# Memory attention and gated convolution: convolution and x by token halves for both head groups side by side, one tap by way of ScalarE and GpSimd

## The chip, the cores and the metric

The kernel runs on one core of one Trainium2 chip. The metric is the device time of one execution in microseconds; the figure for a kernel is the median of its runs.

The core's engines work in parallel, each through a queue of its own in order: TensorE (PE in the profile; PEld is its weight load), VectorE (DVE), ScalarE (ACT), GpSimd (POOL) and SyncE (SP), which issues the transfers. They wait for one another through semaphores. TensorE writes to PSUM, from which VectorE and ScalarE read.

## The reference

Two stages, in float32. The first is an attention through 32 memory slots per head, the second a gated causal convolution of 5 taps with two projections:

```python
# batch 8, heads 8, seq 576, head_dim 64, 32 slots
a = phi - np.max(phi, axis=2, keepdims=True)
a = np.exp(a)
a = a / (np.sum(a, axis=2, keepdims=True) + 1e-09)
k_m = np.einsum('bhsm,bhsd->bhmd', a, k)
v_m = np.einsum('bhsm,bhsd->bhmd', a, v)
scores = scale * np.matmul(q, k_m.transpose(0, 1, 3, 2))
attn = softmax(scores)            # with the same 1e-09
x = np.matmul(attn, v_m)          # heads side by side: (8, 576, 512)
for k in range(5):
    gate_pre += conv_w[k][None, None, :] * xp[:, k:k + S, :]   # xp: x with 4 zero rows ahead
gate = 1.0 / (1.0 + np.exp(-gate_pre))
out = gate * (x @ w_val) @ w_out
```

## The kernel before

The 8 heads are two groups (`g`) of four; the 4 x 32 slots of a group fill the 128 partitions. The 576 tokens are two halves (`s`) of 288. One batch (`b`) passes these steps:

- `load_phi`, `phi_max` to `phi_exp`: the weights of the slots, as exponentials against a common maximum.
- `load_kv`, `slots`: k and v summed into the slots, 20 matmuls for a group; `slots_inv` and `slots_scale` divide by the sum into the tile `kvd`; `slots_turn` and `slots_place` transpose it to `kvT`.
- `scores`, `scores_turn`, `soft_max` to `soft_turn`: the softmax over 32 slots, turned to `pT` (slots on the partitions, tokens along the free dimension, 4 zero columns ahead). `soft_high` and `soft_low` split it into `pH` and `pL`, a rounded value and the rest, for matmuls in a narrower format.
- `val_rows`, `val_high`, `val_low`: v times `w_val`, split into `vwH` and `vwL`. `value(b, s, t)` makes x @ w_val for a half and a pair of heads `t` (0 to 3) by 6 matmuls.
- The gate, in one of two ways. `taps` and `conv(b, g)`: v is multiplied by the five tap weights, and 40 matmuls add the five shifted products in PSUM; `sigmoid` reads them. Or `keep_v` and `mix(b, g)`: 8 matmuls make x itself in PSUM (the tiles `cv`), and `tap(b, t, i)` adds its five shifted, weighted copies into the tile `gate`, tap 0 by ScalarE, taps 1 to 4 by VectorE, each over both halves (576 columns); `open_gate` is the sigmoid. The pairs of batch and group in `MIXED` go the second way: eight of sixteen.
- `gated` multiplies value and gate (tile `h`), `gated_high` and `gated_low` split the product, `project(b, s, n)` multiplies by `w_out` in 12 matmuls, `place` copies the result out of PSUM, `store` sends it.

A matmul of 32 rows by 64 columns takes one of eight parts of TensorE's array. `conv` places the heads of the second half shifted by one head, so that the eight products of (half, head) of a tap lie on eight parts. The heads of that half then lie in another order on the partitions: `swapped` groups need their columns of `vwH` and `vwL` again (`val_again`), and a second copy of `w_out` with its rows in that order (`woH[1]`, `woL[1]`, made by `wo_pair` with transfers inside SBUF). In `mix` both halves use the same four parts, one after the other.

The order of all steps on all engines is the list ORDER, written out in the source; a star behind a name sends the step to the other of its two engines. PSUM is two pools: `cv` (2 tiles of two banks, for `scores`, `conv` and `mix`) and `b` (4 tiles of one bank, for all else). A tile is given out again when its last reader is done. The k and v of a group have one buffer a group (`kvs`); `q` has one for a batch.

Of the kernel before, what the change touches and what calls it, by code (L numbers as in the profile page):

```python
# [721 lines left out]
```

## Time and profile before

| | |
|---|---|
| median of 3 runs | 268.93 us (268.8 to 272.24) |
| the profiled execution | 271.08 us, of which the span from its first to its last instruction 269.3 us |
| mean granted TensorE clock | 0.987 |
| busy: TensorE, VectorE, ScalarE, GpSimd | 250.1, 206.9, 140.5, 116.2 us |
| chain that ended last, by engine | TensorE 83%, transfers 10% |
| moved by transfers | 49.91 MB, 185 GB/s over the span |

All durations below are of the profiled execution and are read against its own 271.08 us. "Busy" counts time in which an engine executes an instruction; matmuls are pipelined, so the mean of one is its latency, and what a series costs is read from the chain of waits, where each piece is the time by which it moves the end. A tensor's line is the line of the helper that issued it: `high` and `low` are lines 216 and 219, `tap` 607 (ScalarE) and 611 (VectorE), `gated` 640, `conv` 577, `mix` 597, `project` 661, `value` 632, `scores` 449, `slots` 403.

### The profile page before, as it was taken

What the parts mean: (1) busy time and instruction counts of PE and PEld (TensorE: products, weight loads), DVE (VectorE), ACT (ScalarE), POOL (GpSimd) and SP (SyncE); (2) the same over time, 40 slices, a digit from 0 to 9 for tenths busy, and PEclk for the clock granted to TensorE, in tenths of its full rate; (3) what the DMA queues carried; (4) which work ended last, traced back from release to release, by engine and by line L of the source; (5) the groups of instructions that cost most, each with busy time, mean ns of one, the idle gap of its engine ahead of it and who ended that gap; (6) DMA issues with size and microseconds to landing.
All of it is one profiled execution on the core that took longest, in us unless ns stands there. A gap on an engine that the chain in (4) does not pass through costs nothing.

```text
span 269.3 us, 7274 instructions
## 1 busy us (share of the span) xinstructions
PE 250.1 (93%) x3096; PEld 216.0 (80%) x3096; DVE 206.9 (77%) x338; ACT 140.5 (52%) x245; POOL 116.2 (43%) x94
## 2 busy tenths in 40 slices
PE   0599959995999999999999999999999999999995
PEld 0387757793988887798789996999879878899994
DVE  2678978996759979789886777789577987898831
ACT  3726764762745558445685346636458565364210
POOL 4466613892921616323635540743237144461200
PEclk9999989998999999999999999999999999999999
DMA  6999987698681992099407268088143210102123
GB/s 203 407 357 355 320 339 247 156 240 234 249 318 60 333 352 99 15 325 347 167 12 217 103 223 267 0 287 334 44 142 127 77 56 2 44 2 88 46 88 131
DMA packets 13232, 49.91 MB, mean 185 GB/s; under 512 B 1673, under 2 KB 2185, under 8 KB 10257
## 3 DMA queue, kind: packets, MB, share of 16 engines
q1 hardware_dynamic: 13200, 49.46, 53.7%
q8 instruction: 24, 0.39, 0.6%
q14 instruction: 8, 0.06, 0.1%
HBM read 37.92 MB, written 9.44 MB: 176 GB/s over the span
## 4 chain that ended last, share of the span: by engine, by line
PE 83%; DMA 10%; issue 2%; ACT 2%; SPq 1%; DVE 1%; DVEq 0%; ACTq 0%
PE b L661 36%; PE b L632 18%; PE cv L577 8%; DMA kv<-in_kv_dram 8%; PE b L403 7%; PE cv L597 4%; PE cv L449 3%; PE b L532 2%; DMA e<-in_phi_dram 2%; PE b L433 2%; PE cv L226 1%; PE b L360 1%; SPq L259 1%; ACT hH L216 1%; DVE h L640 0%
## 5 line engine op out<-in xcount | busy, mean ns | idle before, releaser
L661 PE MATMUL b<-hL,woH 128*128 128x288 f32 x256 | 76.6, 299 | 0.0
L661 PE MATMUL b<-hH,woL 128*128 128x288 f32 x256 | 75.5, 295 | 0.0
L661 PE MATMUL b<-hH,woH 128*128 128x288 f32 x256 | 75.4, 294 | 0.0
L219 POOL TENSOR_TENSOR hL<-h,hH 128x576 fp32r<-128x576 f32 x22 | 32.6, 1488 | 60.0 <-ACT hH L216 32.2
L611 DVE SCALAR_TENSOR_TENSOR gate<-cv,cwP,gate 128x576 f32<-128x576 f32 x64 | 50.0, 813 | 5.9 <-ACT gate L607 4.8
L661 PEld LDWEIGHTS b<-hL,woH 128*128 128x128 f32 x256 | 48.0, 187 | 2.8 <-issue 1.0
L661 PEld LDWEIGHTS b<-hH,woH 128*128 128x128 f32 x256 | 48.2, 188 | 0.0
L661 PEld LDWEIGHTS b<-hH,woL 128*128 128x128 f32 x256 | 48.1, 188 | 0.0
L216 ACT COPY o<-b 128x288 f32<-128x288 f32 x48 | 18.7, 399 | 49.4 <-PE b L661 32.8
L640 DVE TENSOR_TENSOR h<-b,gate 128x288 f32<-128x288 f32 x64 | 27.9, 452 | 19.1 <-PE b L632 15.8
L632 PE MATMUL b<-pL,vwH 128*128 128x288 f32 x128 | 29.0, 308 | 0.0
L632 PE MATMUL b<-pH,vwH 128*128 128x288 f32 x128 | 27.3, 294 | 0.0
L632 PE MATMUL b<-pH,vwL 128*128 128x288 f32 x128 | 27.3, 294 | 0.0
L403 PE MATMUL b<-kv,e 128*32 128x129 f32 x640 | 21.8, 287 | 5.8 <-DMA kv<-in_kv_dram 3.1
L403 PEld LDWEIGHTS b<-kv,e 128*32 128x32 f32 x640 | 18.6, 139 | 8.9 <-issue 4.8
L632 PEld LDWEIGHTS b<-pL,vwH 128*128 128x128 f32 x128 | 20.1, 188 | 6.2 <-issue 2.4
L219 POOL TENSOR_TENSOR pL<-pT,pH 128x1152 fp32r<-128x1152 f32 x7 | 18.7, 2673 | 14.1 <-DVE pH L216 9.8
L577 PE MATMUL cv<-pT,taps 32*64 32x288 f32 x640 | 22.0, 410 | 0.1
L479 POOL TENSOR_TENSOR st<-st,mm 128x1152 f32<-128x1152 f32 x7 | 14.9, 2134 | 15.9 <-DVE mm L472 15.0
L216 ACT CAST hH<-h 128x576 fp32r<-128x576 f32 x21 | 13.9, 673 | 14.0 <-DVE h L640 14.0
L389 POOL TENSOR_TENSOR e<-e,mxa 128x1280 f32<-128x1280 f32 x7 | 17.2, 2464 | 8.7 <-ACT mxa L216 8.7
L632 PEld LDWEIGHTS b<-pH,vwL 128*128 128x128 f32 x128 | 20.5, 188 | 0.0
(87 smaller groups left out, 414.1 us busy)
## 6 DMA issues: line engine op xcount, KB each, us to landing
kv<-in_kv_dram SPq DMA_DIRECT2D x16, 1032.0 KB, 7.6
out_dram<-o SPq DMA_DIRECT2D x30, 288.0 KB, 2.4
q<-in_q_dram SPq DMA_DIRECT2D x7, 1152.0 KB, 8.4
e<-in_phi_dram SPq DMA_DIRECT2D x7, 640.0 KB, 6.4
kv<-in_kv_dram SPq DMA_DIRECT2D x16, 129.0 KB, 8.3
raw<-in_w_out_dram SPq DMA_DIRECT2D x4, 512.0 KB, 8.0
raw<-in_w_val_dram SPq DMA_DIRECT2D x4, 512.0 KB, 6.2
q<-in_q_dram SPq DMA_DIRECT2D x2, 576.0 KB, 8.1
```

The costliest lines, as they stand in the source:

```text
L216: eng.copy(out=out, in_=x) if eng is nc.scalar else eng.tensor_copy(out=out, in_=x)
L219: eng.tensor_tensor(out=out, in0=x, in1=hi.bitcast(F32), op=ALU.subtract)
L389: eng.tensor_tensor(out=t, in0=t, in1=mxa.unsqueeze(3).to_broadcast(list(t.shape)), op=ALU.subtract)
L403: nc.tensor.matmul(km[j * M:(j + 1) * M, 0:2 * D + 1], lhsT=e[:, g, j * M:(j + 1) * M, c], rhs=x[:, c, j, :], start=(c == 0), stop=(c == C ...
L449: nc.tensor.matmul(sc[j * M:(j + 1) * M, s, 0:HALF], lhsT=live["kvT", b, g][rows, 0, j * M:(j + 1) * M], rhs=live["q", b][rows, g, j, :], ...
L479: eng.tensor_tensor(out=st, in0=st, in1=spread(live["mm", b, g], st), op=ALU.subtract)
L577: nc.tensor.matmul(cv[t][x * D:(x + 1) * D, s, 0:HALF], lhsT=w[rows, i, :], rhs=p[rows, g, s * HALF + i:(s + 1) * HALF + i], start=(i == 0 ...
L597: nc.tensor.matmul(cv[t][x * D:(x + 1) * D, s, 0:PAD + HALF], lhsT=live["taps", b, g][rows, 0, :], rhs=pTs[b % 2][rows, g, s * HALF:(s + 1 ...
L611: nc.vector.scalar_tensor_tensor(out=gt, in0=x, scalar=w, in1=gt, op0=ALU.mult, op1=ALU.add)
L632: nc.tensor.matmul(vp[:, 0:HALF], lhsT=a[:, t // PG, n:n + P], rhs=p[:, g, s * HALF:(s + 1) * HALF], start=(i == 0), stop=(i == len(parts) ...
L640: nc.vector.tensor_tensor(out=h[:, i], in0=live["vp", b, s, t][:, 0:HALF], in1=live["gate", b, t][:, s], op=ALU.mult)
L661: nc.tensor.matmul(ps[:, 0:HALF], lhsT=w[:, t, n * P:(n + 1) * P], rhs=a[:, t % 2], start=(i == 0), stop=(i == len(parts) - 1))
```

## The change

`conv(b, s)` and `mix(b, s)` now take one half of the tokens for both groups, where they took one group for both halves. The second group's heads lie shifted by one on the array, for both halves alike; the arrays of weights are laid out in that order of heads ahead of the launch, so `swapped`, `val_again`, the second copies of `w_out` and `wo_pair` go. `kvd` is one tile for both groups, with v of both side by side: `mix` takes its weights there (`keep_v` goes), and three transposes a batch replace four. `tap(b, s, g, i)` works on one half, and as its two tiles of heads have weights of their own it issues two instructions of 288 columns. In the second group tap 1 goes another way: `part_tap` (ScalarE) writes it to a buffer of its own and `join_tap` (GpSimd, once VectorE) adds that to the gate. Twelve pairs of batch and half are mixed now; `conv` is left in 0.0, 0.1, 1.0 and 2.0. The last 64 tokens of k and v of both groups come by one transfer a batch (`load_rest`), and the rest by one for each group, in three buffers in turn. In batch 0 the scores and the softmax go by halves for both groups at once. `scores` has the same eight matmuls per group as before. The gate has 6 buffers instead of 5, `kvd` 3 instead of 2, `st` 2 instead of 1. ORDER is written anew.

```diff
-BUFS = {"raw": 4, "b": 4, "cv": 2, "kvd": 2, "kvT": 3, "st": 1, "vw": 4, "taps": 3, "gate": 5, "h": 3, "hh": 4, "o":
+BUFS = {"raw": 4, "b": 4, "cv": 2, "kvd": 3, "kvT": 3, "st": 2, "vw": 4, "taps": 3, "gate": 6, "h": 3, "hh": 4, "o":
...
-MIXED = {(1, 1), (2, 1), (3, 1), (4, 1), (5, 1), (6, 1), (7, 0), (7, 1)}
+KVS = 3
...
     def load_kv(b, g):
-        t = kvs[g]
-        nc.sync.dma_start(out=t[:, 0:C - 1], in_=kv[b, g, 0:S - KL].rearrange("(p c) n -> p c n", c=C - 1))
-        nc.sync.dma_start(out=t[0:KL, C - 1], in_=kv[b, g, S - KL:])
...
+        t = kvs[(b * G + g) % KVS]
+        nc.sync.dma_start(out=t, in_=kv[b, g])
...
+    def load_rest(b):
+        nc.sync.dma_start(out=rests[b % 2], in_=rest[b])
...
-    def wo_pair(i, g):
...
     def slots_scale(b, g):
...
+        kvd = own(("kvd", b), work, [P, G + 1, 2, D], F32, bufs=BUFS["kvd"])
...
+        for out, x in ((kvd[:, g], km[:, 0:D].unsqueeze(1).to_broadcast([P, 2, D])), (kvd[:, G, g], km[:, D:2 * D])):
...
-    def val_again(b, g, n):
...
-    def conv(b, g):
...
+    def conv(b, s):
+        cv = [psum.tile([P, PG, 512], F32, name="cv", bufs=BUFS["cv"]) for _ in range(G)]
         for i in range(KT):
-            for s in range(2):
+            for g in range(G):
                 for j in range(HG):
-                    rows = slice(j * M, (j + 1) * M)
-                    t, x = divmod((j - s) % HG, 2)
-                    nc.tensor.matmul(cv[t][x * D:(x + 1) * D, s, 0:HALF], lhsT=w[rows, i, :],
-                                     rhs=p[rows, g, s * HALF + i:(s + 1) * HALF + i],
+                    rows, x = slice(j * M, (j + 1) * M), (j + g) % 2
+                    nc.tensor.matmul(cv[g][x * D:(x + 1) * D, j // 2, 0:HALF], lhsT=live["taps", b, g][rows, i, :],
+                                     rhs=pTs[b % 2][rows, g, s * HALF + i:(s + 1) * HALF + i],
                                      start=(i == 0), stop=(i == KT - 1))
...
-    def keep_v(b, g):
...
-    def mix(b, g):
...
+    def mix(b, s):
+        cv = [psum.tile([P, PG, 512], F32, name="cv", bufs=BUFS["cv"]) for _ in range(G)]
+        for g in range(G):
             for j in range(HG):
-                rows = slice(j * M, (j + 1) * M)
-                t, x = divmod(j, 2)
-                nc.tensor.matmul(cv[t][x * D:(x + 1) * D, s, 0:PAD + HALF], lhsT=live["taps", b, g][rows, 0, :],
+                rows, x = slice(j * M, (j + 1) * M), (j + g) % 2
+                nc.tensor.matmul(cv[g][x * D:(x + 1) * D, j // 2, 0:PAD + HALF], lhsT=live["kvd", b][rows, G, g],
                                  rhs=pTs[b % 2][rows, g, s * HALF:(s + 1) * HALF + PAD], start=True, stop=True)
...
+    def tap(b, s, g, i):
+        gt = own(("gate", b, s, g), work, [P, PG, HALF], F32, bufs=BUFS["gate"])
+        for t in range(PG):
+            x, w = live["cv", b, s, g][:, t, i:i + HALF], cwP[:, i, g * PG + t:g * PG + t + 1]
+            if i == 0:
+                nc.scalar.activation(out=gt[:, t], in_=x, func=AF.Identity, scale=w)
+            else:
+                nc.vector.scalar_tensor_tensor(out=gt[:, t], in0=x, scalar=w, in1=gt[:, t], op0=ALU.mult, op1=ALU.add)
+
+    @step
+    def part_tap(b, s, g, i):
+        gt = work.tile([P, PG, HALF], F32, name="gate", bufs=BUFS["gate"])
+        for t in range(PG):
+            nc.scalar.activation(out=gt[:, t], in_=live["cv", b, s, g][:, t, i:i + HALF], func=AF.Identity,
+                                 scale=cwP[:, i, g * PG + t:g * PG + t + 1])
+        live["part", b, s, g, i] = gt
+
+    @step
+    def join_tap(b, s, g, i):
+        gt = live["gate", b, s, g]
+        eng = pick(nc.gpsimd, nc.vector)
+        eng.tensor_tensor(out=gt, in0=gt, in1=live["part", b, s, g, i], op=ALU.add)
```

Before, TensorE's queue around the `mix` of batch 3 (`mx` and `top` belong to the maximum of phi, `kvd` is transposed by `slots_turn`; the brackets name the engine that is waited for):

```order
L360 MATMUL b<-ident,mx 128x128 [waits DVE_49]
L360 MATMUL b<-ident,mx 128x128
L597 MATMUL cv<-pT_76,taps 64x292 [waits DVE_49]
L597 MATMUL cv<-pT_76,taps 64x292 x7
L376 MATMUL b<-ident,top 128x128 [waits DVE_49,Activation_49]
L376 MATMUL b<-ident,top 128x128
L433 MATMUL b<-ident,kvd 128x128 x2
L433 MATMUL b<-ident,kvd 128x128 [waits PE_49]
L433 MATMUL b<-ident,kvd 128x128
```

Now, the same queue around the second `mix` of batch 3; `kv` and `rest` are `slots` of batch 5, `q` the scores of batch 4, `pL` and `pH` belong to `value`:

```order
L395 MATMUL b<-rest_82,e 32x129 x3
L445 MATMUL cv<-q,kvT 32x288 [waits DVE_49]
L445 MATMUL cv<-q,kvT 32x288 x7
L395 MATMUL b<-kv_80,e 32x129 [waits DMAHW0_49]
L395 MATMUL b<-kv_80,e 32x129 x15
L395 MATMUL b<-rest_82,e 32x129 x4
L593 MATMUL cv<-pT_76,kvd 64x292 [waits DVE_49]
L593 MATMUL cv<-pT_76,kvd 64x292 x3
L593 MATMUL cv<-pT_76,kvd 64x292 [waits DVE_49]
L593 MATMUL cv<-pT_76,kvd 64x292 x3
L640 MATMUL b<-pL,vwH 128x288 [waits Activation_49,Pool_49]
L640 MATMUL b<-pL,vwH 128x288
```

The eight matmuls of a `mix` were four and four on the same parts of the array; now they are two fours on other parts, one for each `cv` tile, and each four waits for VectorE's last reading of its tile, here the transposes of the scores, with one `slots` as the work between.

Before, VectorE's queue around the taps of batch 4 (`vwL` and `vwH` are the split of v times w_val for batch 5):

```order
L611 SCALAR_TENSOR_TENSOR gate<-cv,cwP,gate 128x576 [waits Activation_49] x2
L611 SCALAR_TENSOR_TENSOR gate<-cv,cwP,gate 128x576 [waits DVE_49]
L216 COPY o<-b 128x288 [waits DMAHW5_49,DMAHW2_49,PE_49]
L611 SCALAR_TENSOR_TENSOR gate<-cv,cwP,gate 128x576 [waits DVE_49]
L611 SCALAR_TENSOR_TENSOR gate<-cv,cwP,gate 128x576
L611 SCALAR_TENSOR_TENSOR gate<-cv,cwP,gate 128x576 [waits DVE_49] x2
L611 SCALAR_TENSOR_TENSOR gate<-cv,cwP,gate 128x576
L640 TENSOR_TENSOR h<-b,gate 128x288 [waits PE_49,Activation_49]
L219 TENSOR_TENSOR vwL<-b,vwH 128x2x256 [waits Activation_49]
L216 CAST vwH<-b 128x2x256
L219 TENSOR_TENSOR vwL<-b,vwH 128x2x256 [waits DVE_49]
```

Now, the same queue at the two mixes of batch 5 (`pH` is the split softmax, `top` the maximum of phi):

```order
L359 TENSOR_REDUCE top<-b 128x2 [waits PE_49]
L606 SCALAR_TENSOR_TENSOR gate<-cv,cwP,gate 128x288 [waits Activation_49]
L606 SCALAR_TENSOR_TENSOR gate<-cv,cwP,gate 128x288
L606 SCALAR_TENSOR_TENSOR gate<-cv,cwP,gate 128x288 [waits DVE_49] x6
L606 SCALAR_TENSOR_TENSOR gate<-cv,cwP,gate 128x288 [waits Pool_49]
L606 SCALAR_TENSOR_TENSOR gate<-cv,cwP,gate 128x288
L606 SCALAR_TENSOR_TENSOR gate<-cv,cwP,gate 128x288 [waits DVE_49] x4
L648 TENSOR_TENSOR h<-b,gate 128x288 [waits PE_49,Activation_49]
L648 TENSOR_TENSOR h<-b,gate 128x288 [waits PE_49]
L648 TENSOR_TENSOR h<-b,gate 128x288
L606 SCALAR_TENSOR_TENSOR gate<-cv,cwP,gate 128x288 [waits PE_49,Activation_49]
L606 SCALAR_TENSOR_TENSOR gate<-cv,cwP,gate 128x288
```

Eight taps of 576 columns became fourteen of 288 for each `mix`; the last six of them stand behind a wait for GpSimd (the join), and the next `mix` follows behind three products.

Before, SP's queue ahead of the k and v of batch 2 (`kv` with a long and a short transfer for each group; `woL` and `woH` are the copies by `wo_pair`; `e` is phi):

```order
L249 DMA q<-in_q_dram 128x2304 [waits DMAHW7_49,PE_49]
L236 DMA e<-in_phi_dram 128x1280 [waits DMAHW0_49,PE_49,Activation_49]
L241 DMA kv_80<-in_kv_dram 128x2064 [waits DMAHW3_49,DMAHW1_49]
L242 DMA kv_80<-in_kv_dram 64x516 [waits DMAHW4_49,DMAHW2_49]
L339 DMA woL_91<-woL_90 64x1024 [waits Pool_49]
L341 DMA woL_91<-woL_90 64x512
L341 DMA woL_91<-woL_90 64x512 [waits DMAHW5_49]
L339 DMA woH_89<-woH_88 64x1024 [waits DMAHW6_49,Activation_49]
L341 DMA woH_89<-woH_88 64x512 [waits DMAHW7_49]
L341 DMA woH_89<-woH_88 64x512 [waits DMAHW0_49]
L241 DMA kv_78<-in_kv_dram 128x2064 [waits DMAHW1_49]
L242 DMA kv_78<-in_kv_dram 64x516 [waits DMAHW2_49]
```

Now, the same place:

```order
L257 DMA raw<-in_w_out_dram 128x1024 [waits DMAHW4_49,DVE_49]
L247 DMA q<-in_q_dram 128x2304 [waits DMAHW5_49,PE_49]
L237 DMA kv_80<-in_kv_dram 128x2064 [waits DMAHW6_49,DMAHW3_49,PE_49]
L242 DMA rest_81<-in_rest_dram 128x516 [waits DMAHW7_49]
L242 DMA rest_82<-in_rest_dram 128x516 [waits DMAHW0_49,PE_49]
L237 DMA kv_79<-in_kv_dram 128x2064 [waits DMAHW1_49]
L232 DMA e<-in_phi_dram 128x1280 [waits DMAHW2_49,Activation_49]
L682 DMA out_dram<-o 128x576 [waits Activation_49]
```

The copies that waited for ScalarE and GpSimd, with the load of the second group's k and v between them, are gone; both loads of batch 2 now go out ahead of the phi of batch 3 and of the first store.

## Rows read from the trace of the kernel before

**Rows 1.** The page, part 1: busy time, share of the span, instructions.

```profile
PE 250.1 (93%) x3096; PEld 216.0 (80%) x3096; DVE 206.9 (77%) x338; ACT 140.5 (52%) x245; POOL 116.2 (43%) x94
```

**Rows 2.** Busy us (instructions) by engine in five stretches; clock, DMA share, GB/s.

```profile
0.00:23.83 23.83, 13.39 (x113) 10.52 (x113) 14.10 (x23) 11.20 (x20) 12.72 (x19) 1.00 0.91 317
23.83:40.60 16.77, 13.90 (x276) 10.97 (x276) 14.63 (x27) 11.79 (x22) 7.27 (x8) 0.92 0.96 346
40.60:65.87 25.27, 22.49 (x322) 18.72 (x320) 21.29 (x33) 13.82 (x25) 16.03 (x13) 0.97 0.82 211
65.87:266.18 200.31, 200.29 (x2395) 175.74 (x2394) 156.85 (x256) 103.31 (x178) 80.15 (x55) 0.99 0.43 154
266.18:269.30 3.12, 0.00 (x0) 0.00 (x0) 0.00 (x0) 0.40 (x1) 0.00 (x0) 1.00 0.32 113
```

**Rows 3.** Chain of waits: start, us, what.

```profile
53.05 10.82 DMA kv<-in_kv_dram
...
65.87 2.15 PE cv L597 x16
...
123.58 1.14 PE cv L597 x16
...
131.92 1.13 PE cv L449 x32
...
137.28 2.62 PE cv L577 x80
...
153.73 0.22 PE b L433 x2
...
253.37 12.80 PE b L661 x96
```

**Rows 4.** TensorE in order of time, at the k and v of batch 2.

```profile
63.92 1.34 PE L403 MATMUL b<-kv,e 128*32 128x129 f32 x40 [2.78 <-DMA kv<-in_kv_dram]
```

**Rows 5.** Waits of SP's queue: us in total, times, longest.

```profile
SPq L339 <- ACT vwH L216: 7.5, 1, 7.5
```

**Rows 6.** Groups by form: count, busy us, mean ns, idle before and its releasers.

```profile
L611 DVE SCALAR_TENSOR_TENSOR gate<-cv,cwP,gate 128x576 f32<-128x576 f32 x64 | 50.0, 813 | 5.9 <-ACT gate L607 4.8
...
L219 POOL TENSOR_TENSOR hL<-h,hH 128x576 fp32r<-128x576 f32 x22 | 32.6, 1488 | 60.0 <-ACT hH L216 32.2 <-DVE hH L216 12.6 <-PE b L433 9.7
...
L640 DVE TENSOR_TENSOR h<-b,gate 128x288 f32<-128x288 f32 x64 | 27.9, 452 | 19.1 <-PE b L632 15.8 <-ACT gate L616 1.6 <-issue 1.0
...
L216 ACT COPY o<-b 128x288 f32<-128x288 f32 x48 | 18.7, 399 | 49.4 <-PE b L661 32.8 <-issue 15.7 <-ACT mxa L216 0.8
...
L607 ACT ACTIVATE gate<-cv,cwP 128x576 f32<-128x576 f32 x16 | 11.2, 741 | 10.6 <-PE cv L597 10.5
...
L616 ACT ACTIVATE gate<-gate 128x576 f32<-128x576 f32 x16 | 10.9, 687 | 5.6 <-DVE gate L611 5.5
...
L219 DVE TENSOR_TENSOR hL<-h,hH 128x576 fp32r<-128x576 f32 x10 | 7.6, 767 | 0.1
...
L424 DVE TENSOR_SCALAR kvd<-b,ri 128x256 f32<-128x256 f32 x9 | 4.3, 480 | 0.2
```

**Rows 7.** VectorE in order of time, three places: start, us, instruction, count.

```profile
106.82 0.69 DVE L219 TENSOR_TENSOR vwL<-b,vwH 128x512 fp32r<-128x512 f32 x1 [0.51 <-ACT vwH L216]
107.42 0.48 DVE L562 TENSOR_TENSOR taps<-cwB,kvd 128x320 f32<-128x320 f32 x1
...
206.23 0.45 DVE L640 TENSOR_TENSOR h<-b,gate 128x288 f32<-128x288 f32 x1
206.59 0.17 DVE L499 TENSOR_SCALAR ss<-ss 128x36 f32<-128x36 f32 x1
...
236.30 5.88 DVE L611 SCALAR_TENSOR_TENSOR gate<-cv,cwP,gate 128x576 f32<-128x576 f32 x8
```

**Rows 8.** Busy us by engine, as rows 2, in the last 20 us.

```profile
250.00:260.00 10.00, 10.00 (x76) 9.96 (x76) 6.28 (x14) 2.04 (x5) 1.43 (x1) 1.00 0.23 90
260.00:270.00 10.00, 6.16 (x47) 5.92 (x45) 1.59 (x4) 0.40 (x1) 0.00 (x0) 1.00 0.24 89
```

More of the change, by code (lines that the diff above doesn't have):

```diff
@@ L66 @@
-place.0.0.2 slots.2.0 phi_turn.3 slots_scale.2.1* wo_pair.0.0 val_again.1.1.vwH* mix.1.1 slots_inv.2.0 tap.1.2.0
-gated_low.0.1.1 slots_turn.2.1 phi_top.3 phi_spread.3 keep_v.2.1 slots_scale.2.0 soft_high.1* phi_lay.3 tap.1.2.1
-tap.1.2.2 slots_place.2.1 tap.1.3.0 tap.1.2.3 slots_turn.2.0 slots_place.2.0 tap.1.2.4 open_gate.1.2 tap.1.3.1
-tap.1.3.2 soft_low.1 wo_pair.1.1 project.0.1.1 place.0.1.1 load_q.2 project.0.1.0 load_kv.3.0 place.0.1.0 store.0.1.0
-tap.1.3.3 tap.1.3.4 open_gate.1.3 value.1.1.3 project.0.1.2 value.1.1.2 gated.1.1.3 taps.2.0 gated.1.1.2 place.0.1.2*
@@ L81 @@
-project.1.1.1 place.1.1.1 tap.2.2.1 phi_sub.4 phi_exp.4 project.1.0.0 project.1.1.0 place.1.1.0 tap.2.3.2 tap.2.3.3
-project.1.0.2 tap.2.3.4 open_gate.2.3 val_rows.3 place.1.0.2 val_high.3.1 store.1.0.1 tap.2.2.2 tap.2.2.3 tap.2.2.4
-open_gate.2.2 phi_max.5 soft_low.2 place.1.0.0 val_high.3.0 val_again.3.1.vwH conv.2.0 val_low.3.1 taps.3.0*
-val_again.3.0.vwH value.2.0.0 sigmoid.2.0 val_low.3.0 gated.2.0.0 sigmoid.2.1 value.2.0.1 gated.2.0.1 scores.3.0
-scores.3.1 scores_turn.3.0 scores_turn.3.1 soft_max.3 val_again.3.1.vwL* gated_high.2.0.0 slots.4.1 slots_inv.4.1
@@ L91 @@
-tap.3.2.3 tap.3.3.1 load_kv.5.1 tap.3.3.2 tap.3.3.3 store.1.1.0 phi_lay.5 slots_turn.4.1 keep_v.4.1 load_kv.5.0
-slots_turn.4.0 project.2.0.2 tap.3.2.4 project.2.1.3 place.2.0.2 val_again.3.0.vwL* soft_high.3 phi_sub.5
-slots_place.4.0 project.2.1.2 place.2.1.2 load_q.4 project.2.1.0 tap.3.3.4 scores.4.0 slots_place.4.1 scores.4.1
-phi_exp.5 scores_turn.4.0 scores_turn.4.1 soft_max.4 val_rows.4 store.2.0.0 place.2.1.3 store.2.1.1 val_high.4.1*
-place.2.1.0 project.2.1.1 val_high.4.0 taps.4.0* place.2.1.1 open_gate.3.2 soft_low.3 value.3.0.2 val_again.4.0.vwH
@@ L121 @@
-project.5.1.2 val_high.6.1 val_again.6.1.vwH* place.5.1.2 val_low.6.1 value.5.0.3 gated.5.0.3 value.5.0.0 gated.5.0.0
-project.5.1.0 value.5.0.1 soft_exp.6 soft_sum.6 phi_sub.7 phi_exp.7 gated.5.0.1 gated_high.5.0.0 project.5.1.3
-place.5.1.3 soft_inv.6 store.4.1.1 soft_mul.6* soft_turn.6 place.5.1.0* taps.6.0* project.5.1.1 val_again.6.1.vwL
-gated_high.5.0.1 slots.7.0 gated_low.5.0.0 gated_low.5.0.1* slots_inv.7.0 slots_scale.7.0 val_again.6.0.vwL*
-soft_high.6 mix.6.1 slots.7.1 tap.6.2.0 tap.6.2.1 slots_inv.7.1 tap.6.3.0 tap.6.2.2 tap.6.3.1 slots_turn.7.0 load_q.7
@@ new lines @@
+slots_scale.2.1* slots_turn.2 phi_turn.3 slots_place.2 value.1.1.0 join_tap.1.1.1.1 tap.1.1.1.2 tap.1.1.1.3
+tap.1.1.1.4 open_gate.1.1.0 phi_max.4 gated.1.1.1 load_kv.4.0 value.1.0.3 taps.1.0 taps.1.1 phi_top.3 conv.1.0
+sigmoid.1.0.0 load_kv.3.1 gated.1.1.0 sigmoid.1.0.1 taps.2.1 phi_turn.4 phi_top.4 gated_high.1.1.0 load_kv.3.0
+val_rows.2 val_high.2.1 scores.2.0 gated.1.0.3 scores_turn.2.0 scores.2.1 val_low.2.1 phi_spread.3 phi_lay.3 phi_sub.3
+scores_turn.2.1 soft_max.2 open_gate.1.1.1 project.0.1.0 project.0.1.1 place.0.1.0* val_high.2.0 val_low.2.0
```

400 lines of the change are left out of this document (205 added, 195 removed).

## The prediction

> **What bounds the kernel now.** I read the page's engine shares first [rows 1]: TensorE is busy 93% of the span, VectorE 77%, ScalarE 52%, GpSimd 43%. A share is an average, so next came a table of five stretches [rows 2]. From 65.87 to 266.18 us TensorE is busy 200.29 of 200.31 us at a granted clock of 0.99, and before that it has gaps. VectorE is busy 156.85 us of the same stretch, so it idles 43.5. The chain of waits [rows 3] says the same: from the first `mix` at 65.87 to the last projection that ends at 266.17 it runs through TensorE alone. So a microsecond taken from TensorE in that stretch is a microsecond of the end, as long as nothing else becomes late. Ahead of it the chain runs through loads, the last of them kv from 53.05 us on, and 3.1 us lie behind it.
>
> **TensorE, what goes.** In the chain one `conv` takes 2.62 us, one `mix` 1.14, and the scores of both groups 1.13 [rows 3]. A `conv` issues 40 matmuls and lays its eight (half, head) products of one tap on eight different parts of the array. A `mix` issues only 8, but its two token halves use the same four parts, so it takes two rounds of four. The scores are the model for what follows: 8 matmuls of 288 columns on eight parts, 1.13 / 2 = 0.57 us.
> - `conv` now takes both groups for one half: again 40 matmuls on eight parts, so again 2.62 us. In the stretch there were six (batches 1 to 6), now there are two (1.0 and 2.0): 4 x 2.62 = 10.5 us less.
> - `mix` now has both groups on eight parts: 0.57 us by the scores; the bounds are 0.52 (two of conv's ten rounds) and 1.14 (nothing gained). There were 8, now 12: 8 x 1.14 = 9.1 becomes 12 x 0.57 = 6.8, so 2.3 less.
> - The transposes of `slots_turn` fall from four to three a batch, 0.22 us for two [rows 3]: 0.11 a batch over some six batches, 0.7 less.
> Together 13.5 us, and the stretch needs 200.3 - 13.5 = 186.8 us of TensorE. Projections, values and slots keep their number.
>
> **The head.** I expect the first `mix` at about 63 instead of 65.87 us. TensorE waits 2.78 us at 61.1 for the kv of batch 2 [rows 4]. Its load goes out only at 53.05 [rows 3], since SP's queue stood 7.5 us at a copy of `woH` or `woL` that waited for ScalarE [rows 5]. Those twelve copies are gone, a kv tile has three buffers instead of one per group, and the order shows both kv loads of batch 2 ahead of anything that waits for late work. Against it: the first softmax needs the queries of both groups now, and they stand behind nine other loads. VectorE's work up to the first `mix` is about as long as before. I take the 2.8 us off; the bounds are 6 off and 1 on. What would be late next there is VectorE, busy 21.29 of 25.27 us in the stretch from 40.60 [rows 2].
>
> **VectorE, what comes.** This is the price of the change. A `mix` now serves one half of both groups: per mix 8 + 6 taps of 288 columns, since each tile of heads has weights of its own; 12 x 14 = 168 replace 64 of 576 columns (50.0 us) [rows 6]. No row shows a 288-column tap. Eight in a row of 576 take 5.88 us, 0.735 each [rows 7]. From below: half of that is 0.37. From above: the 288-column product `h`, which also reads PSUM, takes 0.452 by its mean [rows 6]. In between: `vwL`, 512 columns, starts 0.60 us ahead of its successor, and `h`, 288, 0.36 [rows 7], so a column costs 1.07 ns, and 0.735 - 288 x 1.07 ns = 0.43 us. I take 0.43, since it is from the tap itself: 168 x 0.43 = 72 us (62 to 76).
>
> [...]
>
> Less work elsewhere, by the order's counts: seven `hL` differences move from VectorE to GpSimd (7 x 0.767 = 5.4), nine `kvd` scalings of 0.48 become four smaller ones in the first two batches (about 3) [rows 6], and some ten small copies, casts and products go (0 to 5, I take 4). So VectorE needs 156.9 - 50.0 + 72 - 12 = 167 us in the stretch, where TensorE needs 186.8.
>
> **Does VectorE keep up?** Behind the last `mix` VectorE is nearly done while TensorE still has some 10 us more of work than VectorE has (the last 12.8 us are projections alone [rows 3]). So VectorE has 186.8 - 10 = 177 us for its 167: it may idle 10 us. Before it idled 43.5, of which 19.1 in front of `h`, mostly for TensorE's values [rows 6]; some 8 of the rest lay behind 250 us [rows 8]. If it still has to wait those 19.1, TensorE waits 9 us for gates; if less than 10, nothing. I take the middle, **4.5 us**; the bounds are 0 and 9.
>
> **ScalarE and GpSimd** are hidden. ScalarE gets 48 + 24 first and part taps in place of 16 (72 x 0.40 by the 288-column copy `o`, less 16 x 0.741: +17 us), 8 more sigmoids of 0.69 against 8 fewer behind `conv`, and the `kvd` scalings: some 125 of 187 us [rows 2, 6]. GpSimd gets 11 joins and 7 `hL`, 18 x 1.49 = 27 us, and loses the copies of `val_again` and `keep_v`: about 105 of 187. They count only as a delay: the second group's gate passes from ScalarE (tap 0 and the part tap) to GpSimd's join and back to six VectorE taps, while both `cv` tiles stay taken. In VectorE's order the first group's eight taps stand ahead of the wait for the join. They start behind the first of three pairs of ScalarE steps and end 0.8 + 3.4 = 4.2 us into the mix; the three pairs and the join take 2.4 + 1.5 = 3.9. So the join is covered, just, where nothing else is queued on GpSimd; its longest other work there is a `pL` or a subtraction, which could add 1 to 2 us to VectorE's waiting and is part of the bound of 9.
>
> **The sum.** Head 63.1, stretch 186.8 + 4.5, end 3.1: a span of 257.5 us. The profiled execution took 271.08 us with a span of 269.30, so 1.8 lie around it: 259.3. It was itself 0.8% above the median of 268.93: 259.3 x 268.93 / 271.08 = **257 us** on the scale of the median, 4.4% less. Its own range: 250 (VectorE hidden, head 3 us quicker) to 262 (VectorE waits as before).
>
> **Rivals.**
> A. VectorE becomes the bound. It keeps the whole of its old waiting outside the tail (35 us) beside 167 us of work: 202 instead of the 177 it has, so TensorE loses 25 us instead of 4.5. With half of that excess the span is 257.5 + 10 = 267.5 and the time 267. For it: in the stretch VectorE would be busy 89%, and it works its queue in order, so each wait for a value holds up the next taps. Against it: several batches are in work at once, and before the change it filled 78% without holding TensorE up once. [...]
> B. Slower: the hold on the `cv` tiles. There are two, a `mix` takes both, and the next `mix` or scores waits until the last tap has read them. The tail of a mix is 0.57 + three pairs of ScalarE taps 2.4 + a join 1.49 + six taps 2.6 = 7.1 us, and between the two mixes of batch 5 TensorE has only some 6.4 us of other work; with VectorE's other work among the taps the wait is 1 to 2 us. At 2 us on each of 12 mixes the span is 253 + 24 = 277 and the time 277. It decides from (269.3 - 253) / 12 = 1.4 us per mix. Against it: by the order, what follows most mixes on `cv` are scores, which take the first group's tile; it is free after 4.2 us, and TensorE has 4 us or more of values and projections ahead of them.
> C. The groups don't run side by side: `mix` stays at 1.14 and each `conv` takes 5.2. That adds 12 x 0.57 + 4 x 2.6 = 17 us: 274. Against it: the eight products differ in rows or columns of the array exactly as `conv`'s did.
>
> **How the numbers follow.** Chances: forecast 0.76, A 0.14, B 0.04, C 0.03, and 0.03 for a head much quicker than thought (under 250). The two slow cases and the fast one are left out of the range, and A is taken in: 250 to 268. A measurement of this kernel can tell about 2%, so the bounds are 263.6 and 274.3: faster 0.80, same 0.14, slower 0.06.
>
> **What would show it.** Right: `mix` groups of 16 records at about 0.55 us, taps near 0.43 apart and 168 of them, VectorE busy near 220 us in all, TensorE without long gaps behind the first `mix`, and no wait for kv at 60 us. Wrong: `mix` at 1.1 (C); TensorE idle ahead of `mix` or scores and released by VectorE's taps (B), or ahead of projections and released by gates and `hL` (A); a first `mix` behind 66 us (the head). The likeliest error is the 4.5 us, since it is a choice between two bounds.

## The result and the profile after

The changed kernel takes 258.44 us (median of 4 runs, 257.58 to 261.12) beside 270.59 for the kernel before on the same chip: ratio 0.959, 95% interval 0.947 to 0.971. The ratio leaves out the one slow run of the kernel before (273.93 us). A second, longer comparison of the same kernel gave 0.961 (0.956 to 0.965). The forecast was 257 us. The profiled execution took 257.97 us with a span of 256.2; the forecast for the span was 257.5.

The page, part 1, of the kernel after (as [rows 1]):

```profile
PE 235.5 (92%) x2788; PEld 201.6 (79%) x2788; DVE 215.4 (84%) x418; ACT 164.8 (64%) x309; POOL 135.8 (53%) x94
```

The table of stretches of the kernel after, cut where its first `mix` begins and its last projection ends (as [rows 2]):

```profile
34.30:61.17 26.87, 25.68 (x432) 22.06 (x432) 24.42 (x38) 18.75 (x34) 21.10 (x13) 1.00 0.49 187
61.17:252.97 191.80, 190.26 (x2134) 167.00 (x2134) 169.53 (x343) 127.74 (x243) 102.07 (x60) 1.00 0.44 158
252.97:256.20 3.23, 0.00 (x0) 0.00 (x0) 0.00 (x0) 0.40 (x1) 0.00 (x0) 0.92 0.32 113
```

The span fell from 269.3 to 256.2: 4.7 us in the head (the first `mix` at 61.17 instead of 65.87), 8.5 in the stretch (200.31 to 191.80), and nothing in the end. VectorE now idles 22.3 us of the stretch where it idled 43.5 [rows 2].

The chain of waits of the kernel after: start, us, what.

```profile
57.50 2.12 DVE st L517
...
59.64 1.38 DVE pT L523
...
63.03 2.71 DVE gate L606 x7
...
66.02 2.28 DVE gate L606 x6
...
69.22 2.66 PE cv L580 x72
...
88.68 0.68 PE cv L593 x16
...
243.31 9.61 PE b L669 x72
```

Up to 69 us the chain runs mostly through VectorE: softmax of batch 1, then thirteen taps and one more, then the `conv` that waits for their tile. Before, loads stood there [rows 3]. Behind it TensorE has the chain, but for one piece of VectorE from 103 to 110 us.

Groups by form of the kernel after (as [rows 6]):

```profile
L606 DVE SCALAR_TENSOR_TENSOR gate<-cv,cwP,gate 128x288 f32<-128x288 f32 x168 | 74.2, 507 | 4.4 <-ACT gate L604 1.5 <-POOL gate L620 1.3 <-PE b L640 1.1
...
L648 DVE TENSOR_TENSOR h<-b,gate 128x288 f32<-128x288 f32 x64 | 27.1, 445 | 6.2 <-PE b L640 4.7 <-ACT gate L625 1.4
...
L620 POOL TENSOR_TENSOR gate<-gate 128x576 f32<-128x576 f32 x11 | 15.8, 1437 | 24.1 <-ACT gate L604 19.5 <-ACT gate L612 4.6
```

A tap of 288 columns costs 74.2 / 168 = 0.442 us on the mean; in the row of nine shown below it takes 3.91 / 9 = 0.434. The waiting in front of `h` fell from 19.1 [rows 6] to 6.2 us, although VectorE works more. A likely reading: it had been early for TensorE's values, and now it comes later and finds them ready.

**Waits inside a busy group.** TensorE's queue in order of time, at two mixes and at `conv.1.0`:

```profile
68.34 0.71 PE L580 MATMUL cv<-pT,taps 32*64 32x288 f32 x8
69.22 2.66 PE L580 MATMUL cv<-pT,taps 32*64 32x288 f32 x72 [0.17 <-DVE gate L606]
...
161.93 0.75 PE L593 MATMUL cv<-pT,kvd 32*64 32x292 f32 x16
...
169.10 1.37 PE L593 MATMUL cv<-pT,kvd 32*64 32x292 f32 x16
170.40 0.40 PE L640 MATMUL b<-pL,vwH 128*128 128x288 f32 x1
```

And VectorE's, beside the second of these mixes:

```profile
165.78 3.91 DVE L606 SCALAR_TENSOR_TENSOR gate<-cv,cwP,gate 128x288 f32<-128x288 f32 x9
```

Both mixes have 16 records (two a matmul), but the second takes 1.30 us to the next instruction, not 0.68: its second half needs the tile that VectorE reads until 165.78 + 3.91 = 169.69. Three mixes (at 120.76, 143.55 and 169.10 us) take 1.05, 0.94 and 1.30, together 1.25 more than three of 0.68; and `conv.1.0`'s first eight records take 0.88 us to the next where a tenth of 2.62 is 0.26. No idle row names most of this. With the 1.5 us of idle rows (0.17 and 0.95 for VectorE, 0.36 with no releaser named), TensorE waits about 3.2 us in the stretch, some 2.8 of it for VectorE, and its own work is 188.6.

### The profile page after: what moved, and what is told of

The parts are those of the page before. It is cut to its first block, busy times and chain, and to the rows that moved or that the text cites. A ratio compares the mean times of both kernels' runs of the same rounds, so it can differ in the third digit from the quotient of the medians.

```text
span 256.2 us, 6798 instructions
## 1 busy us (share of the span) xinstructions
PE 235.5 (92%) x2788; PEld 201.6 (79%) x2788; DVE 215.4 (84%) x418; ACT 164.8 (64%) x309; POOL 135.8 (53%) x94
## 4 chain that ended last, share of the span: by engine, by line
PE 71%; DVE 16%; DMA 6%; ACT 2%; issue 2%; SPq 1%; POOL 1%; ACTq 0%; POOLq 0%
PE b L669 37%; PE b L640 17%; PE b L395 5%; PE cv L593 3%; PE cv L445 3%; DMA q<-in_q_dram 3%; DMA raw<-in_w_val_dram 3%; PE b L545 2%; DVE gate L606 2%; DVE st L517 2%; DVE pT L523 2%; DVE ss L501 2%; DVE ss L510 1%; DVE hH L299 1%; DVE st L490 1%
## 5 line engine op out<-in xcount | busy, mean ns | idle before, releaser
L606 DVE SCALAR_TENSOR_TENSOR gate<-cv,cwP,gate 128x288 f32<-128x288 f32 x168 | 74.2, 507 | 4.4 <-ACT gate L604 1.5
L215 POOL TENSOR_TENSOR hL<-h,hH 128x576 fp32r<-128x576 f32 x29 | 41.8, 1450 | 46.8 <-ACT hH L212 24.3
L212 ACT COPY o<-b 128x288 f32<-128x288 f32 x50 | 19.6, 402 | 38.0 <-PE b L669 27.3
L620 POOL TENSOR_TENSOR gate<-gate 128x576 f32<-128x576 f32 x11 | 15.8, 1437 | 24.1 <-ACT gate L604 19.5
L604 ACT ACTIVATE gate<-cv,cwP 128x288 f32<-128x288 f32 x48 | 21.3, 513 | 4.4 <-PE cv L593 4.4
L215 POOL TENSOR_TENSOR pL<-pT,pH 128x1152 fp32r<-128x1152 f32 (+1 forms) x8 | 20.1, 2508 | 4.3 <-ACT pH L212 4.3
L290 POOL TENSOR_TENSOR hH<-hH,hL 128x512 int32<-128x512 int32 (+1 forms) x9 | 11.9, 1329 | 17.7 <-DVE hH L276 10.3
L381 POOL TENSOR_TENSOR e<-e,mxa 128x1280 f32<-128x1280 f32 x6 | 15.9, 2654 | 8.9 <-ACT mxa L212 8.9
L640 PEld LDWEIGHTS b<-pH,vwH 128*128 128x128 f32 x128 | 20.5, 188 | 0.0
L395 PEld LDWEIGHTS b<-kv,e 128*32 128x32 f32 x512 | 14.8, 140 | 6.4 <-ACT e L386 2.0
```

What stands on the lines that cost most here:

```text
L212: eng.copy(out=out, in_=x) if eng is nc.scalar else eng.tensor_copy(out=out, in_=x)
L215: eng.tensor_tensor(out=out, in0=x, in1=hi.bitcast(F32), op=ALU.subtract)
L290: nc.gpsimd.tensor_tensor(out=a, in0=a, in1=r, op=ALU.add)
L381: eng.tensor_tensor(out=t, in0=t, in1=mxa.unsqueeze(3).to_broadcast(list(t.shape)), op=ALU.subtract)
L395: nc.tensor.matmul(km[j * M:(j + 1) * M, 0:2 * D + 1], lhsT=e[:, g, j * M:(j + 1) * M, c], rhs=x[:, c, j, :] if c < C - 1 else rests[b % 2 ...
L604: nc.scalar.activation(out=gt[:, t], in_=x, func=AF.Identity, scale=w)
```

## The experiments

Ratios are to the kernel before on the same chip. "To after" is the difference of the ratio to after's 0.961, times 270 us.

| kernel | edit | ratio, 95% interval | span | to after |
|---|---|---|---|---|
| e0 | after, again | 0.961 (0.956 to 0.965) | 259.5 | |
| e1 | no part tap, no join | 0.980 (0.976 to 0.985) | 262.0 | +5 |
| e2 | second group not shifted | 1.001 (0.999 to 1.004) | 267.5 | +11 |
| e3 | without tap 4 | 0.949 (0.944 to 0.954) | 255.4 | -3 |
| e4 | before, taps in two | 1.009 (1.005 to 1.014) | 271.4 | |
| e5 | before, no copies | 0.993 (0.990 to 0.997) | 266.8 | |
| e6 | tap 0 by VectorE | 1.044 (1.039 to 1.050) | 280.6 | +23 |
| e7 | five places of TensorE's order | 0.988 (0.984 to 0.993) | 266.0 | +7 |
| e8 | extra full matmuls | 1.011 (1.003 to 1.019) | 268.4 | +13 |
| e9 | extra small matmuls | 1.048 (1.041 to 1.056) | 280.8 | +24 |
| e10 | two parts | 1.131 (1.124 to 1.137) | 301.4 | +46 |
| e12 | two parts, second join by VectorE | 1.057 (1.048 to 1.066) | 282.7 | +26 |

The theory ("TensorE theory") was that TensorE's shorter queue is the gain and VectorE's longer one still fits beside it; the rival ("VectorE theory"), that VectorE now sets the time. Beside them the changed kernel ran again, unaltered:

> The changed kernel unaltered, as the measure for the runs beside it. Both theories: 0.955 to 0.965 of the kernel before, span 256 to 259 us. TensorE theory: from the first mix on (61 us), TensorE sets the end, since conv and mix now fill eight parts of its array; VectorE has some 8 us of slack. VectorE theory: VectorE (busy 170 of 192 us there, and on the chain up to 69 us) sets the pace, and each microsecond of its work moves the end.

It came out at 259.64 us, the first `mix` at 62.47 us and the same three long mixes. From there to its last projection it took 193.80 us, where the first profile has 191.80: single profiles of one kernel differ by that much.

**e2, the array.** The second group's heads go to the same four parts as the first's:

```diff
-rows, x = slice(j * M, (j + 1) * M), (j + g) % 2
+rows, x = slice(j * M, (j + 1) * M), j % 2
```

> The second group's heads are not shifted, so both groups use the same four of the eight parts in conv and mix; the gate of that group gets its heads in pairs exchanged. Nothing else differs. TensorE theory: a mix goes from 0.68 to about 1.2 us in the chain and a conv from 2.65 to 5.2, so 12 x 0.5 + 4 x 2.6 = 16 us more, nearly all of it at the end, since VectorE is not the bound: span 269 to 273, the time of the kernel before. VectorE theory: TensorE has room, +0 to +6 us (span 256 to 262).

The whole gain is gone: 270.18 us. Groups by form of e2, `conv` and `mix`, then the same of after:

```profile
L580 PE MATMUL cv<-pT,taps 32*64 32x288 f32 x320 | 20.3, 403 | 0.7 <-DVE pT L523 0.7
...
L593 PE MATMUL cv<-pT,kvd 32*64 32x292 f32 x192 | 14.6, 417 | 1.2 <-DVE ri L402 1.2
```

```profile
L580 PE MATMUL cv<-pT,taps 32*64 32x288 f32 x320 | 11.5, 406 | 0.7 <-DVE pT L523 0.4 <-DVE gate L606 0.2
...
L593 PE MATMUL cv<-pT,kvd 32*64 32x292 f32 x192 | 10.2, 429 | 1.8 <-DVE pT L523 1.0 <-DVE ri L402 0.8
```

Busy time on these grows by 8.8 + 4.4 = 13.2 us; the span grows by 11.3, since TensorE's waits go (it is busy 198.64 of 198.66 us of e2's stretch). A `mix` is back at 1.14, a `conv` takes 5.0. So side by side on eight parts is what the change lives on, and rival C's price was right in kind: I had 17 us.

**e3 and e1, VectorE less and more.** e3 leaves out tap 4 of all gates (48 VectorE instructions):

```diff
-... tap.1.1.0.3 tap.1.1.0.4 ...
+... tap.1.1.0.3 ...
```

> Tap 4 is left out in all twelve mixes, so 48 VectorE instructions of 0.44 us go, 21 us of VectorE's work behind the first mix; all else stays. TensorE theory: TensorE idles only 1.5 us there, so the end moves by 1 to 4 us (span 252 to 255). VectorE theory: by 12 to 21 us (span 235 to 244). My forecast's term of 4.5 us for TensorE's waiting on VectorE would come back in full if it was of the right size.

It gave back 3.2 us for 21 us of VectorE work by the count (18.8 by the tables of the stretch): the TensorE theory. The table of stretches of e3, from its first `mix`:

```profile
61.83:252.20 190.37, 188.08 (x2134) 166.11 (x2134) 150.78 (x295) 127.27 (x243) 101.92 (x60) 1.00 0.44 159
```

All its twelve mixes take 0.68 to the next instruction and both its convs of the stretch 2.61. So most of the 2.2 us that TensorE's busy time lost (190.26 to 188.08) were waits for VectorE, as read above.

e1 undoes the way by ScalarE and GpSimd:

```diff
-part_tap.1.1.1.1 ... join_tap.1.1.1.1 tap.1.1.1.2
+... tap.1.1.1.1 tap.1.1.1.2
```

> Undoes the second part of the change alone: tap 1 of the second group goes by VectorE again, in the place of the join; the tap by ScalarE and the addition by GpSimd are gone. VectorE gets 24 instructions of 0.44 us and loses one addition: +9.8 us in the stretch behind the first mix. TensorE theory: VectorE's slack of 177 - 169.5 = 7.5 us takes most of it, so +0 to +4 us against the changed kernel (span 256 to 260). VectorE theory: +8 to +10 us (span 264 to 266).

5 us more for 9.8 us of VectorE work (9.0 by the pages, 215.4 to 224.4), between the theories. TensorE's waits in e1 (engine, line, releaser: us, times, longest) name VectorE's taps where after has a single 0.2:

```profile
PE cv L579 <- DVE gate L605: 1.0, 1, 1.0
...
PE cv L592 <- DVE gate L605: 0.8, 1, 0.8
PE cv L444 <- DVE gate L605: 0.8, 1, 0.8
```

**e6, VectorE much more.** Tap 0 goes to VectorE too:

```diff
-nc.scalar.activation(out=gt[:, t], in_=x, func=AF.Identity, scale=w)
+nc.vector.tensor_scalar(out=gt[:, t], in0=x, scalar1=w, scalar2=None, op0=ALU.mult)
```

> The changed kernel with tap 0 of all 24 gates by VectorE instead of ScalarE: 48 more VectorE instructions of 0.44 us, 21 us more VectorE work, some 23 us less of ScalarE's. This measures the other side of leaving out tap 4. VectorE idles 22 us in the stretch. TensorE theory (only what does not fit counts): VectorE would need 169.5 + 20 = 190 us where TensorE needs 190, it cannot be packed that tightly, 4 to 10 us more than after, 264 to 270 us. VectorE theory (every microsecond counts): 21 us more, 281. From the experiment with 9.8 us more VectorE work, which cost 5, I expect more than half: some 14 us, 274.

282.44 us, 22.6 more, for 19.5 us more of VectorE's busy time in the stretch (169.53 to 189.03). My guess of two thirds was wrong; the number is that of the VectorE theory. The stretch of e6, and of it the part ahead of the last 21 us:

```profile
61.92:277.40 215.48, 199.90 (x2134) 170.45 (x2134) 189.03 (x391) 110.61 (x196) 102.21 (x60) 0.98 0.39 141
61.92:256.50 194.58, 179.90 (x1990) 151.14 (x1990) 177.56 (x365) 105.69 (x185) 97.93 (x57) 0.98 0.41 149
```

The same part of after:

```profile
61.17:232.00 170.83, 169.35 (x1979) 146.33 (x1980) 158.10 (x318) 123.33 (x234) 97.78 (x57) 1.00 0.47 169
```

VectorE is not full by its busy time, yet it sets much of the time: it has 37% of the chain that ended last in e6, 16% in after. Ahead of the last 21 us it idles 17.0 us in e6, 12.7 in after. What it idles there it does not get rid of.

Not all of the 22.6 us is VectorE's length. ScalarE's and TensorE's queues of e6, and the table of stretches behind TensorE's wait (the clock is the third number from the end):

```profile
190.70 0.89 ACT L612 ACTIVATE gate<-cv,cwP 128x288 f32<-128x288 f32 x2 [7.26 <-DVE gate L604]
```

```profile
194.23 1.12 PE L395 MATMUL b<-kv,e 128*32 128x129 f32 x32 [3.30 <-ACT e L386]
```

```profile
194.00:198.00 4.00, 3.77 (x50) 3.48 (x51) 2.01 (x6) 0.18 (x1) 1.97 (x1) 0.66 0.93 308
```

A part tap stands 7.26 us in ScalarE's queue for VectorE's tap 0, with the exponentials of phi behind it. TensorE waits 3.30 us for these, and behind that wait the granted clock was 0.66 over 4 us. How much of the 22.6 us is VectorE's added work and how much the order of ScalarE's queue, no run separates.

**e4, the same load where VectorE has room.**

```diff
-nc.vector.scalar_tensor_tensor(out=gt, in0=x, scalar=w, in1=gt, op0=ALU.mult, op1=ALU.add)
+for s in range(2):
+    nc.vector.scalar_tensor_tensor(out=gt[:, s], in0=x[:, s], scalar=w, in1=gt[:, s], op0=ALU.mult, op1=ALU.add)
```

> The kernel before with each of its 64 taps of 576 columns issued as two VectorE instructions of 288, as the change does, and nothing else. By the rows of after a tap of 288 takes 0.442 us, so VectorE gets 64 x (0.884 - 0.735) = 9.5 us more. TensorE theory (before the change VectorE had 43.5 us of idle time in the stretch, so its added work is free): within 1 us of before, 270 us. VectorE theory (each added microsecond of VectorE counts): 279 us. It also gives the price of a tap of 288 columns outside the changed kernel: two in a row should be 0.88 us, or 0.74 if splitting costs nothing.

2.5 us more (1.3 to 3.7). Its 128 taps are busy 55.5 us in all, where 64 were busy 50.0 [rows 6]: 5.5 us of VectorE work (8.5 beside 64 taps in a row of 0.735 [rows 7]). So it is not free, though VectorE idled 43.5 us there: the last `mix`, where no other work stands between, now waits for the taps, in TensorE's queue of e4:

```profile
242.57 2.05 PE L597 MATMUL cv<-pT,taps 32*64 32x292 f32 x16 [0.22 <-DVE gate L612]
244.82 0.40 PE L662 MATMUL b<-hL,woH 128*128 128x288 f32 x1 [0.20 <-ACT o L216]
```

It is 2.25 us from the first to the second, where before the same mix had 1.27. That is 1.0 of the 2.1 us between the two spans.

**e5, the head.** The kernel before without the twelve copies of `woH` and `woL`:

```diff
-(w[s if swapped(b, t // PG) else 0], live[a, b, s, t // 2], t)
+(w[0], live[a, b, s, t // 2], t)
```

> The kernel before without its twelve copies of woH and woL; the projections of the swapped heads use the unswapped weights, so the output is another. Their place in SP's queue is all that goes. My forecast took 2.8 us off the head for the kv loads of batch 2 that stood behind them. If those copies were the cause: the load of kv goes out some 7 us earlier, the wait of 2.78 us at 61 us is gone, the first mix starts at 63 instead of 65.9, and the time falls by 2.8 us (1%) to 267.5. Rival: another wait, for VectorE, is nearly as late there, and only 0 to 1 us is gained; then the 4.7 us of the changed kernel's head come from the side by side work and not from the queue.

0.7% less (0.3 to 1.0), 1.8 us, and 2.5 in the span. The first `mix` starts at 64.26 us, released by VectorE (0.80 us), and the wait for kv is gone. Where the wait's price lay is shown by the table of stretches of the kernel before, behind the end of that wait (the clock is the third number from the end), and by the first `mix` of e5 in TensorE's queue.

```profile
66.00:68.00 2.00, 2.00 (x17) 0.64 (x13) 1.40 (x3) 0.00 (x0) 0.52 (x1) 0.50 0.98 413
...
63.92:68.75 4.83, 4.83 (x63) 2.97 (x64) 1.80 (x5) 1.00 (x3) 1.79 (x3) 0.65 0.86 298
```

```profile
64.26 1.21 PE L589 MATMUL cv<-pT,taps 32*64 32x292 f32 x16 [0.80 <-DVE ri L402]
```

Before, behind the idle 2.78 us, the granted clock was 0.65 over 4.83 us, and the first `mix` took 2.15 [rows 3], here 1.15. So by these rows the kv wait cost its own 2.8 and, as an estimate, 4.83 x 0.35 = 1.7 more. Only 2.5 of these 4.5 us come back, since a wait for VectorE is next.

The head was counted by the start of the first `mix`. There the copies make 1.6 of its 4.7 us (65.87 to 64.26). The other 3.1 us were not tested, but the tables of stretches up to the first `mix`, before and after, show less work for VectorE, whose `ri` releases the first `mix` of after:

```profile
0.00:65.87 65.87, 49.78 (x706) 40.21 (x708) 50.02 (x82) 36.81 (x66) 36.02 (x39) 0.97 0.89 284
```

```profile
0.00:61.17 61.17, 45.23 (x655) 34.59 (x655) 45.86 (x76) 36.62 (x66) 33.73 (x34) 0.94 0.74 281
```

VectorE is busy 4.2 us less. e0 and e3 fit that (46.8 us of VectorE's work, first `mix` at 62.47 and 61.83), and so does e5 (49.4 and 64.26). VectorE is not alone there: e2, with 46.7, whose `conv.0.0` and `conv.0.1` take 2.4 us longer each, starts its first `mix` at 65.64.

**e7, mixes a little later.** TensorE's order altered at five places, one of them:

```diff
-open_gate.5.1.0 phi_spread.7 gated_high.4.1.0 mix.5.0 soft_low.5 gated.4.0.2 value.5.1.3 gated.4.1.3
+open_gate.5.1.0 phi_spread.7 gated_high.4.1.0 soft_low.5 gated.4.0.2 value.5.1.3 mix.5.0 gated.4.1.3
```

> The changed kernel with TensorE's order altered at five places, the same work on every engine: three mixes that start before VectorE has read the second cv tile (at 120.8, 143.6 and 169.1 us their 16 records take 1.05, 0.94 and 1.30 us instead of 0.68) go behind the next value or val_rows, conv.1.0 (3.5 instead of 2.6 us) goes behind a transpose, and mix.3.1, which waits 0.95 us for soft_turn, goes behind slots_turn and a projection. If those are waits for VectorE inside TensorE's busy time: 1.25 + 0.7 + 0.95 = 2.9 us at most come back, 2 to 3 us less than after, 257 us. Rival: VectorE sets the pace there and the wait only moves to the next step that needs a gate: 0 to 1 us.

Both theories fall: 267.35 us, 7 us more. The mixes' waits did go (8.1 us for all twelve instead of 9.4, from start to next start), but TensorE now idles 8.4 us behind its first `mix`, and `conv.1.0` takes 4.0 us where it had 3.5. TensorE's waits in e7:

```profile
PE b L347 <- DVE h L643: 2.5, 1, 2.5
...
PE cv L440 <- DVE gate L601: 1.3, 1, 1.3
PE b L420 <- DVE h L643: 1.2, 1, 1.2
PE b L635 <- ACT mxa L207: 1.0, 1, 1.0
```

The transposes that I moved ahead need a `b` tile that a product `h` still reads, and that product stands in VectorE's queue among the taps. The scores behind a later `mix` wait for its taps. I had looked at what the moved steps read, not at the tile that they write.

**e8 and e9, full and small tiles.** One useless matmul of 32 columns ahead of each of 64 projections, in e8 on the full array, in e9 on a 32x64 part:

```diff
+nc.tensor.matmul(ps[:, 320:352], lhsT=ident, rhs=ident[:, 0:32], start=True, stop=True)
...
+nc.tensor.matmul(ps[0:D, 320:352], lhsT=ident[0:M, 0:D], rhs=ident[0:M, 0:32], start=True, stop=True)
```

> The changed kernel with one useless matmul of 128x128 by 32 columns ahead of each of the 64 projections, into columns of the projection's bank that nobody reads. It is the reference for the next kernel: the same, but on 32x64 parts. A transpose of 128 columns takes 0.11 to 0.14 us by the rows of after, so this one should take 0.03 to 0.1 us: 2 to 6 us more than after in all, 262 to 266 us.

> As the kernel before it, but the useless matmul sits on a 32x64 part of the array instead of all of it. My reading of the mis-sized mix (0.68 us each where half of a pair of scores gave 0.57): going from full tiles to small ones and back costs TensorE about 0.2 us a visit, since scores that are followed by other small tiles take 0.51 and those followed by full tiles 0.65, and the first full tile behind them 0.24 instead of 0.13. If so: 64 x 0.2 = 13 us more than the 128x128 twin. Rival: the mix is simply longer and a visit costs nothing: the same as the twin, or less, within 2 us.

e8 costs 13 us, 0.2 each, more than I thought; e9 10 us more than e8 (ratios 1.048 and 1.011), that is 0.16 us a visit of the small part. TensorE's queue in e8, then in e9:

```profile
228.82 0.31 PE L666 MATMUL b<-ident 128*128 128x32 f32 x2
228.96 0.38 PE L670 MATMUL b<-hL,woH 128*128 128x288 f32 x1
229.18 0.29 PE L670 MATMUL b<-hH,woL 128*128 128x288 f32 x1
```

```profile
227.29 0.29 PE L670 MATMUL b<-hH,woH 128*128 128x288 f32 x1
227.51 0.30 PE L666 MATMUL b<-ident 32*64 32x32 f32 x2
227.74 0.40 PE L670 MATMUL b<-hL,woH 128*128 128x288 f32 x1
227.97 0.30 PE L670 MATMUL b<-hH,woL 128*128 128x288 f32 x1
```

In e8 the extra takes 0.14 us, and the first projection matmul behind it 0.22 instead of 0.13, on the full array too. In e9 the matmul ahead of the extra takes 0.22, the extra 0.23 and the one behind it 0.23. The projection's operands are in the narrower format and the extra's are not; whether that is the cause wasn't tried.

**e10 and e12, more of the same medicine.** Tap 4 of the first group also by ScalarE and GpSimd:

```diff
-part_tap.1.1.1.1 tap.1.1.0.1 ... tap.1.1.0.3 tap.1.1.0.4
+part_tap.1.1.1.1 part_tap.1.1.0.4 tap.1.1.0.1 ... tap.1.1.0.3 join_tap.1.1.0.4
```

> The changed kernel with a second tap moved off VectorE: tap 4 of the first group's gates also goes by ScalarE into a buffer and is added by GpSimd, at the place in the order where VectorE's tap 4 stood (a seventh gate buffer for it). VectorE loses 24 x 0.442 = 10.6 us, ScalarE gets 24 x 0.45 = 11, GpSimd 12 x 1.45 = 17; both have over 60 us of room in the stretch. Leaving tap 4 of both groups out gave back 3.2 us for 21 us of VectorE work. TensorE theory: 0 to 2 us less than after, 257.5 to 259.5. Rival: the join comes last in a gate's chain and takes 1.45 us where two taps took 0.88, and GpSimd's queue delays it further, so that products wait for gates: 2 to 6 us more, 261.5 to 265.5.

303.82 us: 46 more, though VectorE has less to do. Of these, 12.8 us are in TensorE's busy time (248.3 us instead of 235.5, for the same work), at a mean granted clock of 0.938 instead of 0.986. GpSimd's queue of e10 at the first of these joins, and TensorE's:

```profile
68.46 1.40 POOL L515 TENSOR_TENSOR gate<-gate 128x576 f32<-128x576 f32 x1 [9.62 <-DVE gate L501]
69.81 1.40 POOL L110 TENSOR_TENSOR hL<-h,hH 128x576 fp32r<-128x576 f32 x1
```

```profile
71.27 0.61 PE L564 MATMUL b<-hL,woH 128*128 128x288 f32 x1 [8.27 <-POOL hL L110]
```

GpSimd stands 9.6 us for VectorE's taps with an `hL` behind it, for which a projection waits 8.3. e12 gives only the new joins to VectorE:

```diff
-join_tap.1.1.0.4
+join_tap.1.1.0.4*
```

> The kernel with two parts again, but the twelve joins of tap 4 of the first group are VectorE's (one instruction of 576 columns, 0.75 us by the one such row of after, instead of two taps of 0.44). With the second join on GpSimd the time was 303.8 us, 44 more than after; GpSimd stood 9.6 us in front of the first of these joins for VectorE's taps, and the hL behind it in its queue held up a projection for 8.3 us. Theory (GpSimd's queue, that is the place of the join in front of hL): back to 258 to 261 us, VectorE having 12 x 0.14 = 1.7 us less work than in after. Rival (ScalarE's 24 more part taps delay its other steps): stays above 285.

284.9 us: 20 of the 46 go with the joins' place in GpSimd's queue. My theory explains less than half. For the rest the waits, and no run, point at ScalarE's part taps. VectorE's waits in e12, and its queue at the first `mix`:

```profile
DVE gate L501 <- ACT gate L507: 24.9, 12, 4.7
```

```profile
66.16 2.64 DVE L501 SCALAR_TENSOR_TENSOR gate<-cv,cwP,gate 128x288 f32<-128x288 f32 x6 [1.69 <-ACT gate L507]
```

VectorE's first tap waits until ScalarE's four part taps have passed, 24.9 us in twelve places; in after it starts 0.02 us behind tap 0, at 63.03. Whether it is the shared `cv` tile or the order of the semaphore's counts that ties it to the part taps was not tried. e6 shows a like wait the other way round: there a part tap waits 7.26 us for VectorE's tap 0 on the same `cv` tile, whose result it doesn't read. The joins are also dearer than I had put them: e12's thirteen on VectorE are busy 15.4 us, 1.18 each and not 0.75, so VectorE has more work than in after (220.7 us, 215.4).

## Why the prediction was right, point by point

- **TensorE's sum.** 186.8 us forecast, 188.6 measured. The step that was mis-sized is the `mix`: 0.57 us "by the scores", that is half of a pair. It is 0.68, 12 x 0.11 = 1.3 us more. The half pair left out what a visit to small tiles costs at its ends, which a pair pays once (in after one visit of scores takes 0.65 us to the next instruction, at 93.95 us, and a pair 1.10, at 73.06): by e9's 0.16 us that is, as an estimate, 0.08 of the 0.11, and the rest is open. `conv` was right at 2.62 (2.61). The other 0.5 us was not taken apart.
- **TensorE waiting for VectorE, 4.5 us.** Some 2.8 measured (3.2 with the row that names no releaser), within the bounds of 0 and 9. The working was that VectorE may idle 10 us ahead of the tail. It idles 12.7 there. Its old 19.1 us in front of `h` fell to 6.2, so the upper bound, which kept them, was not a bound that could come true as such.
- **The stretch.** 186.8 + 4.5 = 191.3 against 191.8 (193.8 in e0): the two errors cancel. As the 4.5 was the middle of two bounds, that they do is luck; the step that carries the forecast, both groups side by side, is shown by e2.
- **The head.** 63.1 forecast, 61.2 and 62.5 in two profiles. The kv wait did go (no row at 60 us, both loads out at 38.6 and 39.9 us), and what is late next is VectorE, as said. But "I take the 2.8 us off" is not what the copies were worth by themselves: e5 starts its first `mix` only 1.6 us sooner. And "VectorE's work up to the first `mix` is about as long as before" was wrong: it is 4.2 us less (3.2 in e0). The two errors have opposite signs.
- **VectorE.** 167 us forecast in the stretch, 169.5 measured; the tap 0.442 on the mean, not 0.43, which makes 2.0 of the 2.5. In a row, which is what the 0.43 was taken from, it is 0.434.
- **ScalarE and GpSimd.** 127.7 and 102.1 us, forecast 125 and 105, and hidden. The join is covered "just": 1.3 us of waits for it in 168 taps. e10 shows how little more it takes.
- **Rival A** did not come, but stood close. Less VectorE work gives back some 15% of it (e3), 9.8 us more cost half (e1), 21 us more cost all (e6, with ScalarE's queue in it). So the price of VectorE work rises about where the change lies.
- **Rival B**'s hold on `cv` exists: three mixes and a `conv` show it, some 1.9 us in all and not 24. **Rival C** is e2, and did not happen.
